# A gate's sum moved out of a prologue: ScalarE and GpSimd take it over beside the second half of v, and GpSimd alone splits the weight pieces

## The chip, the cores and the metric

The kernel runs on one core of one Trainium2 chip. The metric is the device time of one execution in microseconds (us). The engines, as the profile names them: PE is TensorE's matmuls and PEld its weight loads, DVE is VectorE, ACT is ScalarE, POOL is GpSimd, and SP is SyncE, which here only issues DMAs. Each engine runs its own instructions strictly in the order in which the program holds them, so an instruction that waits holds up everything behind it on that engine; this is the thing to keep in mind in what follows.

## The reference

Two attention blocks run on the same input x (2048 x 1024, f32), one linear (A) and one softmax (B), each with 32 heads of 32 columns, and a gate mixes them row by row:

```python
x = A_x
g = _sigmoid((x * gate_w).sum(-1, keepdims=True))
a = _A_ref(x, A_wqkv, A_wo)     # linear attention, then @ wo
b = _B_ref(x, B_wqkv, B_wo)     # softmax attention, then @ wo
return g * a + (1 - g) * b
```

The change concerns two small parts of it. One is g: a weighted sum over the 1024 columns of x, for each of 2048 rows. The other is a preparation of `B_wo`: sums and differences of its quarters, each of them split in two parts.

## The kernel before, in words

All matmuls take f32 numbers split in a high part (a cast to fp32r) and a low part (the rest), with three matmuls per product: high by high, high by low, low by high. `split` makes both parts: ScalarE casts, another engine subtracts. So each operand costs one ScalarE and one VectorE instruction of 128x512.

The program has two ages. In the **prologue** all orders are written by hand. It goes through x in two halves, J = 0 and J = 1. For each half, `v_pass` makes the first half of v for B (8 steps k, banks 0 to 7), and then eight calls of `quad` make q and k for B by a scheme with seven instead of eight products per 2x2 block (`product(0)` to `product(6)`, 12 matmuls each, in six PSUM banks in turn). VectorE joins the products (L494, L501 to L503, L507, L508, L511) and splits results and weights (L294). While one quad runs, `quad_weights` builds the seven weight operands of the next one in a ring of `RINGW` places (12 before). `load_quad` fetches raw weights for the quad after that. After every product `quad` calls `next(side)`, and that is one **turn** for everything that runs beside it:

- `quad_weights`, a step per turn;
- `spill_rest`, which writes x's parts to memory for later (tiles xs);
- `gate_`, the generator `gate()`: for each of 4 column blocks j and 8 row blocks k it loads a 128x512 tile of x into the one buffer `gate_x` (SyncE), two turns later multiplies it by a column of weights and adds it to `gate_sum` (VectorE, L376 for the first k, L378 for the other seven), and after eight of these sums over the partitions by four small matmuls with `ones` (L381);
- `parts`, the generator `wo_parts()`: 28 pieces of B's output weights. GpSimd loads raw tiles by its own DMA queue (L526), ScalarE casts the high part (L534), GpSimd subtracts for the low part (L535), and GpSimd stores both (L537). A piece starts every `PIECE_STEP` = 4.1 turns.

`gate_x`, `gate_sum` and the raw pieces lie in the big tile 15; the pieces' parts in `zrep`. What `gate()` has not finished when the last quad but one of J = 1 ends, it finishes there in one go (`for _ in gate_: pass`).

Then comes the **main loop**. From here on a planner in Python chooses, instruction by instruction, what PE does next, by modelled times `T`; `use` books a cost on an engine, `T["pe"]` is 0 at its start. It begins with the second half of v (16 units of 24 matmuls, each unit loading x's parts again as xh<-xs and big<-xs), beside the first head's maxima; then come the heads, in which PE, VectorE and GpSimd are all close to full.

Of the kernel before, what the change touches and what calls it, by code (L numbers as in the profile page):

```python
# [11 lines left out]
F32R = mybir.dt.float32r  # L12
AF = mybir.ActivationFunctionType
# [6 lines left out]
P = 128  # L20
# [19 lines left out]
NE = 3  # L40
AHEAD_X = 3
PIECE_STEP = 4.1
LATE = 1.0
MANUAL = {ET.PE, ET.DVE, ET.Activation, ET.SP, ET.Pool}
NMID = 13
# [3 lines left out]
def kernel(  # L49
# [34 lines left out]
    def f32r(ap):  # L84
        return ap.bitcast(F32R)
# [34 lines left out]
    def big_tile(i, dtype):  # L120
        return sb.tile([P, S], dtype, name=f"big{i}")

    big = [None if i in (15, 16, 17) else big_tile(i, F32R) for i in range(NBIG)]
# [42 lines left out]
    def dma(to, of):  # L166

        T["sp"] = max(T["sp"], T["pe"]) + DMA_ISSUE
        nc.sync.dma_start(to, of)  # L169
# [140 lines left out]
    for side in PLACES:  # L310
        side["X12"] = side["T4"]
    NQB = 6
    RINGW = [(18, 0), (18, 1), (19, 0), (19, 1), (14, 0), (14, 1), (20, 0), (20, 1), (17, 0), (17, 1), (16, 0),
             (16, 1)]
    NP = len(PRODUCTS)
    QUADS = 2 * NK // 2
    assert NK == 8 and NPAIR == 2
# [21 lines left out]
    def halves(t):  # L339
        return [t[:, i * C:(i + 1) * C] for i in range(t.shape[1] // C)]  # L340

    RAW_BIG = (17, 16, 15)
    assert not {b for b, _ in RINGW[:NK]} & set(RAW_BIG)
    raw_big = [halves(big_tile(b, F32)) for b in RAW_BIG]
    raw_a = [mid[5], extra] + halves(sb.tile([P, 2 * HK * P], F32, name="xh"))
# [13 lines left out]

    def vcols(c):  # L360
        return [(2 * D + c * C, C)]

    z0, z1, gate_sum, gate_x = raw_w0
    gate_wt = mneg[:, :NK]

    def gate():

        yield
        for j in range(NJ):
            for k in range(NK):  # L370
                dma(gate_x, xT[k * P:(k + 1) * P, j * C:(j + 1) * C])
                yield
                yield
                w = gate_wt[:, k:k + 1]
                if k == 0:
                    nc.vector.tensor_scalar_mul(gate_sum, gate_x, w)  # L376
                else:
                    nc.vector.scalar_tensor_tensor(gate_sum, gate_x, w, gate_sum, op0=ALU.mult, op1=ALU.add)  # L378
                yield
            for i in range(TPC):  # L380
                nc.tensor.matmul(bank[7][:, i:i + 1], gate_sum[:, i * P:(i + 1) * P], ones[:, :1], start=True, stop=True)  # L381
            nc.scalar.activation(g_sb[:, j * TPC:(j + 1) * TPC], bank[7][:, :TPC], AF.Exp, scale=-1.0)
        nc.vector.tensor_scalar_add(g_sb, g_sb, 1.0)
        nc.vector.reciprocal(g_sb, g_sb)
        nc.vector.tensor_scalar(omg_sb, g_sb, -1.0, 1.0, op0=ALU.mult, op1=ALU.add)

    gate_ = gate()

    def load_x(raws, J, jj, k, c0=0, c1=C):
        j = 2 * J + jj  # L390
# [54 lines left out]
    def quad_weights(raws, J, f):  # L445

        w11, w12, w21, w22 = raws

        def part(s, raw):
            n = quad_ring(J, f, s)  # L450
            split(ring_w(n, 0), ring_w(n, 1), raw, nc.vector)

        part(0, w11)
        yield
        part(6, w22)
        nc.vector.tensor_add(w22, w21, w22)
        yield
        nc.vector.tensor_sub(w21, w11, w21)
        part(1, w12)
        nc.vector.tensor_sub(w11, w22, w11)  # L460
        yield
        part(3, w22)
        nc.vector.tensor_sub(w12, w12, w11)
        yield
        part(4, w11)
        part(2, w12)
        yield
        part(5, w21)
# [49 lines left out]

    def wo_parts():

        hi_w, lo_w = (f32r(z) for z in halves(zrep))
        at, turn = [1.0], count()

        def load(z, m, i, **add):
            if i < KH:
                nc.gpsimd.dma_start(z, wo_piece(m, i), **add)  # L526

        def wait():
            at[0] += PIECE_STEP
            while next(turn) + 1 < at[0]:  # L530
                yield

        def part(m, i, z):
            nc.scalar.copy(hi_w, z)  # L534
            nc.gpsimd.tensor_sub(lo_w, z, f32(hi_w))  # L535
            for p, src in enumerate((hi_w, lo_w)):
                nc.gpsimd.dma_start(wo_d[m][p][:, i * C:(i + 1) * C], f32(src))  # L537

        yield
        load(z1, "W11", 0)  # L540
        load(z0, "W21", 0)
        yield from wait()
        for i in range(KH):
            part("W11", i, z1)
            nc.gpsimd.tensor_sub(z1, z1, z0)
# [22 lines left out]
    parts = wo_parts()  # L568

    def halves_of(t):  # L570
        return [t[:, i * D:(i + 1) * D] for i in range(2)]
# [74 lines left out]
    for k in range(NK):  # L646
# [16 lines left out]
        if k == 6:  # L663
            for _ in spill(0, "X12"):
                pass
    for i, b in enumerate((16, 17)):
        w_t[i] = big[b] = big_tile(b, F32R)
    quad_w = quad_weights(raw_a, 0, 0)
    for _ in range(3):
        next(quad_w)  # L670
# [6 lines left out]

    def change():

        load_wv_again(range(NK - 3))  # L680
        split_x(raw_x1[0], 1, 0, 0)
        yield
        load_wv_again([NK - 3])
        split_x(raw_x1[0], 1, 1, 0)
        yield
        load_wv_again([NK - 2])
        split_x(raw_x1[0], 1, 0, 1)
        yield
        load_wv_again([NK - 1])
# [12 lines left out]
    for k in range(NK):  # L702
# [310 lines left out]
    def linear():  # L1013
        extra = iter(())
        for n, (i, t) in enumerate(units):
# [64 lines left out]
            if kind == "v":  # L1080
                give(b, use("act", 0.5, T["pe"] + LATENCY["pe"]))
                v_out(c, token(i, t), ps, mid[11 - n % 2])
            elif kind == "kv":
                va = mid[7][:, (n % 2) * HC:(n % 2 + 1) * HC]
                yield from keys_alone(n - 2)
                nc.scalar.copy(va, ps[:, HC:])
# [732 lines left out]
    while streams or tasks:  # L1819
        if not begun[0] and lin_done[0] >= warm and s_done[0] >= NT * NJ + LEAD:  # L1820
            begun[0] = True
            advance("head")
        pump_w()
        fold_now()
        add_now()
        load_w_op()
        fill(T["pe"] + SLACK)
        task = next((i for i, (start, _) in enumerate(tasks)
                     if start() is not None and start() <= T["pe"]), None)
        if task is not None:  # L1830
# [36 lines left out]
        advance(name)  # L1867
        goal[0] += (st_done[0] - before) * rates[lin_kind[0]]
# [24 lines left out]
```

## Time and profile before

| | |
|---|---|
| Median of 3 runs | 2891.49 us (2888.26 to 2895.98) |
| Profiled execution | 2892.11 us, of which the span of the profile is 2890.3 us |
| Granted TensorE clock, mean | 0.989 |
| Share of the span busy | PE 98%, DVE 81%, POOL 70%, ACT 56% |
| Bytes moved | 459.51 MB, mean 159 GB/s |

How to read it: a window row gives, for a stretch of time, each engine's busy time and in brackets its number of instructions, then the granted clock and the mean busy share of the 16 DMA engines. A row of the waits says who waited, for whom, how long in total, how many times, and the longest. PE's records overlap, since matmuls are pipelined; so PE's count in a stretch says more than its busy time. The prologue lies between 0 and some 480 us, the second half of v between 480 and 590 us, and the heads follow.

### The profile page before, as it was taken

The page shows a single profiled execution, that of the slowest core. Times are in us where ns is not written, and L with a number is a line of the kernel's source. Part 1 is how long each engine was busy: PE and PEld are TensorE (multiplying, and loading weights), DVE is VectorE, ACT ScalarE, POOL GpSimd, SP SyncE. Part 2 cuts the span into 40 slices and gives each one's busy share as a digit, 9 for nine tenths or more (in the row PEclk, how much of TensorE's full clock was granted, in tenths as well). Part 3 has the DMA queues.
Part 4 walks back from the last instruction along what each step waited for, and adds up shares of the span by engine and source line. Part 5 has one row for each costly group of instructions (what it writes and reads, how often), then busy time and mean ns, then how long its engine had stood idle before and what let it go on. Part 6 is the DMA issues. An engine that isn't in the chain of part 4 may idle for free.

```text
span 2890.3 us, 46884 instructions
## 1 busy us (share of the span) xinstructions
PE 2819.5 (98%) x15880; PEld 2055.3 (71%) x15880; DVE 2341.8 (81%) x3777; ACT 1630.6 (56%) x3063; POOL 2036.4 (70%) x1066
## 2 busy tenths in 40 slices
PE   9798888999999999999999999999999999999999
PEld 8677777876777677667766777777767666676677
DVE  7777665688888888888888888888888888887678
ACT  5334322066667566666666666666666666665522
POOL 0323303069899999999999999789989988888000
PEclk9899999999999999999999999999999999999999
DMA  8888876643443334434443344446656554644775
GB/s 278 268 255 272 271 217 200 186 137 105 101 126 103 95 96 119 114 98 108 113 116 92 96 108 133 151 152 201 189 172 198 153 155 112 173 116 131 249 245 156
DMA packets 403338, 459.51 MB, mean 159 GB/s; under 512 B 106894, under 2 KB 234894, under 8 KB 401308
## 3 DMA queue, kind: packets, MB, share of 16 engines
q1 hardware_dynamic: 381084, 419.03, 48.2%
q0 software_dynamic: 22016, 37.50, 6.0%
q8 instruction: 126, 2.06, 0.3%
q14 instruction: 112, 0.92, 0.1%
HBM read 314.31 MB, written 127.66 MB: 153 GB/s over the span
## 4 chain that ended last, share of the span: by engine, by line
PE 84%; DMA 7%; DVE 5%; issue 2%; ACT 2%; SPq 1%; POOL 0%; ACTq 0%; DVEq 0%
PE bank L1350 16%; PE bank L1208 16%; PE bank L1500 15%; PE bank L152 11%; PE bank L155 11%; PE bank L157 11%; DMA big<-in_xT 2%; DVE big L294 2%; DMA qk<-mid 1%; ACT mid L293 1%; SPq L169 1%; DVE mid L294 1%; DMA xh<-in_b_wqkv 1%; PE bank L1272 1%; DMA v<-mid 1%
## 5 line engine op out<-in xcount | busy, mean ns | idle before, releaser
L1435 POOL TENSOR_TENSOR big<-big,big 128x512 f32<-128x512 f32 (+2 forms) x694 | 1642.5, 2371 | 107.5 <-ACT big L1353 64.8
L1213 DVE TENSOR_REDUCE mx<-bank 128x1 f32<-128x512 f32 x2048 | 1313.4, 683 | 297.4 <-PE bank L1208 294.0
L1353 ACT ACTIVATE big<-bank 128x512 f32<-128x512 f32 x2048 | 1180.5, 602 | 429.3 <-PE bank L1350 363.2
L1350 PE MATMUL bank<-big,big 128*128 128x512 f32 x1888 | 741.5, 394 | 2.2 <-DMA big<-ml 1.6
L1208 PE MATMUL bank<-big,big 128*128 128x512 f32 x1888 | 739.2, 392 | 1.7 <-ACT big L1353 1.7
L152 PE MATMUL bank<-big,big 128*128 128x512 f32 x1576 | 625.2, 397 | 33.9 <-DVE mid L503 21.3
L155 PE MATMUL bank<-big,big 128*128 128x512 f32 x1576 | 621.7, 394 | 1.3 <-DVE big L294 1.1
L157 PE MATMUL bank<-big,big 128*128 128x512 f32 x1572 | 619.4, 394 | 0.3 <-DMA big<-xs 0.2
L1500 PE MATMUL bank<-big,mid 128*32 128x512 f32 x4096 | 454.2, 593 | 0.0
L1350 PEld LDWEIGHTS bank<-big,big 128*128 128x128 f32 x1888 | 354.0, 188 | 127.2 <-issue 47.0
L1208 PEld LDWEIGHTS bank<-big,big 128*128 128x128 f32 x1888 | 354.5, 188 | 75.7 <-ACT big L1353 3.4
L152 PEld LDWEIGHTS bank<-big,big 128*128 128x128 f32 x1576 | 300.7, 191 | 104.4 <-issue 24.5
L155 PEld LDWEIGHTS bank<-big,big 128*128 128x128 f32 x1576 | 300.8, 191 | 65.4 <-DVE big L294 2.3
L157 PEld LDWEIGHTS bank<-big,big 128*128 128x128 f32 x1572 | 299.3, 190 | 65.7 <-DMA big<-xs 1.2
L1500 PEld LDWEIGHTS bank<-big,mid 128*32 128x32 f32 x4096 | 143.5, 110 | 264.4 <-issue 264.1
L1451 DVE TENSOR_TENSOR bank<-bank,big 128x512 f32<-128x512 f32 x364 | 251.8, 692 | 5.2 <-ACT big L1353 2.9
L535 POOL TENSOR_TENSOR zrep<-big,zrep 128x512 fp32r<-128x512 f32 x28 | 40.6, 1449 | 230.3 <-ACT zrep L534 191.7
L293 ACT CAST mid<-mid 128x512 fp32r<-128x512 f32 x64 | 39.7, 620 | 207.9 <-DVE mid L503 103.2
L1431 POOL TENSOR_TENSOR big<-big,big 128x1536 f32<-128x1536 f32 (+1 forms) x31 | 123.2, 3975 | 40.6 <-ACT big L1353 40.4
L294 DVE TENSOR_TENSOR big<-mid,big 128x512 fp32r<-128x512 f32 (+1 forms) x157 | 111.8, 727 | 47.3 <-ACT big L293 47.1
L152 PE MATMUL bank<-big,xh 128*128 128x512 f32 x376 | 147.1, 391 | 0.7 <-DVE mx L1213 0.7
L293 ACT CAST big<-mid 128x512 fp32r<-128x512 f32 (+1 forms) x157 | 92.7, 617 | 96.0 <-DVE mid L1619 66.0
(154 smaller groups left out, 2284.1 us busy)
## 6 DMA issues: line engine op xcount, KB each, us to landing
big<-xs SPq DMA_DIRECT2D x288, 256.0 KB
big<-qk SPq DMA_DIRECT2D x690, 64.0 KB
xh<-xs SPq DMA_DIRECT2D x144, 256.0 KB
qk<-mid SPq DMA_DIRECT2D x128, 256.0 KB
big<-oA SPq DMA_DIRECT2D x84, 256.0 KB
xs<-big SPq DMA_DIRECT2D x64, 256.0 KB
oA<-mid SPq DMA_DIRECT2D x64, 256.0 KB
big<-big POOLq DMA_DIRECT2D x50, 256.0 KB, 5.5
```

The source lines that it names most:

```text
L152: yield nc.tensor.matmul(ps, sh, mh_, start=(kt == 0), stop=False)
L155: yield nc.tensor.matmul(ps, sh, ml_, start=False, stop=(late and last))
L157: yield nc.tensor.matmul(ps, sl, mh_, start=False, stop=last)
L293: nc.scalar.copy(hi, src)
L294: eng.tensor_sub(lo, src, f32(hi))
L1208: nc.tensor.matmul(bank[b], q[:, t % TPC * P:(t % TPC + 1) * P], k[:, j * C:(j + 1) * C], start=True, stop=True)
L1213: nc.vector.tensor_reduce(m[:, t, j:j + 1], bank[b], AX.X, ALU.max)
L1350: nc.tensor.matmul(bank[b], k[:, t * P:(t + 1) * P], q_cols(h, j), start=True, stop=True)
L1353: nc.scalar.activation(pr_t[i][:, j * C:(j + 1) * C], bank[b], AF.Exp, scale=SCALE)
L1435: nc.gpsimd.tensor_add(lacc[:, sl], lacc[:, sl], pr(t)[:, sl])
L1451: nc.vector.tensor_add(lacc[:, qp:] if t == NT - 1 else l_b[:, :n], l_b[:, :n], src)
L1500: nc.tensor.matmul(av_b[j * DH:(j + 1) * DH, :], v[:, t, :], pr(t)[:, j * C:(j + 1) * C], start=(t == 0), stop=(t == NT - 1))
```

## The change

Two steps move.

1. `gate()` goes. Its work is done by `gate_step()`, which the main loop calls once per decision: from `T["pe"]` = 8.0 on, one step each 2.5 modelled us, 32 steps. A step loads a tile of x (SyncE) into one of four buffers; 8 us later ScalarE multiplies it by its weight column, and GpSimd adds it to one of two sums. The matmuls with `ones` remain, four groups of four, as tasks of the planner.
2. In a piece, GpSimd casts the high part itself. ScalarE only writes one column of a small tile, from which GpSimd copies, so that a piece still starts where it did. The raw tiles move to `zrep`, the parts to half of big 15; that frees one more place for the ring `RINGW`, which becomes 13 long.

With the longer ring `quad_weights` makes its operands up to a turn earlier: operand 6 and the sum behind it in the first turn, and so on. And the reload of the v weights (`load_wv_again`) takes six instead of five steps in its first turn.

```diff
-    RINGW = [(18, 0), (18, 1), (19, 0), (19, 1), (14, 0), (14, 1), (20, 0), (20, 1), (17, 0), (17, 1), (16, 0),
-             (16, 1)]
+    RINGW = [(16, 0), (16, 1), (17, 0), (17, 1), (19, 0), (19, 1), (14, 0), (14, 1), (20, 0), (20, 1), (15, 0),
+             (18, 0), (18, 1)]
...
-    RAW_BIG = (17, 16, 15)
+    RAW_BIG = (20, 15, 18)
...
-    def gate():
-        yield
-        for j in range(NJ):
-            for k in range(NK):
-                dma(gate_x, xT[k * P:(k + 1) * P, j * C:(j + 1) * C])
-                yield
-                yield
-                w = gate_wt[:, k:k + 1]
-                if k == 0:
-                    nc.vector.tensor_scalar_mul(gate_sum, gate_x, w)
-                else:
-                    nc.vector.scalar_tensor_tensor(gate_sum, gate_x, w, gate_sum, op0=ALU.mult, op1=ALU.add)
-                yield
-            for i in range(TPC):
-                nc.tensor.matmul(bank[7][:, i:i + 1], gate_sum[:, i * P:(i + 1) * P], ones[:, :1], start=True, stop=True)
...
         part(0, w11)
-        yield
         part(6, w22)
         nc.vector.tensor_add(w22, w21, w22)
         yield
         nc.vector.tensor_sub(w21, w11, w21)
         part(1, w12)
+        yield
         nc.vector.tensor_sub(w11, w22, w11)
+        part(3, w22)
         yield
-        part(3, w22)
         nc.vector.tensor_sub(w12, w12, w11)
+        part(4, w11)
         yield
-        part(4, w11)
         part(2, w12)
...
-        hi_w, lo_w = (f32r(z) for z in halves(zrep))
+        z0, z1 = halves(zrep)
+        hi_w, lo_w = (big[15][:, i * C:(i + 1) * C] for i in (2, 3))
...
         def part(m, i, z):
-            nc.scalar.copy(hi_w, z)
+            n = next(tokens) % (C // DH)
+            nc.scalar.copy(dn[0][:, n:n + 1], eps)
+            nc.gpsimd.tensor_copy(dn[1][:, n:n + 1], dn[0][:, n:n + 1])
+            nc.gpsimd.tensor_copy(hi_w, z)
             nc.gpsimd.tensor_sub(lo_w, z, f32(hi_w))
...
+    gate_wt = omg_sb[:, :NK]
+    gate_n, gate_at, gate_busy = [0], [GATE_FROM], deque()
+    gate_x = [mid[7], mid[8], mid[9], zrep[:, :C]]
+    def gate_step():
+        while gate_busy and min(gate_busy)[0] <= T["pe"]:
+            first = min(gate_busy)
+            gate_busy.remove(first)
+            first[-1]()
+        n = gate_n[0]
+        if n >= NJ * NK or gate_at[0] > T["pe"]:
+            return
+        gate_n[0] += 1
+        gate_at[0] = T["pe"] + GATE_STEP
+        j, k = divmod(n, NK)
+        raw, acc = gate_x[n % len(gate_x)], (mid[6], zrep[:, C:])[j % 2]
+        assert all(at[1] > n - len(gate_x) for at in gate_busy)
+        dma(raw, xT[k * P:(k + 1) * P, j * C:(j + 1) * C])
+        def times():
+            use("act", 0.62, T["pe"])
+            nc.scalar.activation(raw if k else acc, raw, AF.Copy, scale=gate_wt[:, k:k + 1])
+            if k:
+                plus()
+        def plus():
+            end = use("pool", 1.3, T["act"] + LATENCY["act"])
+            nc.gpsimd.tensor_add(acc, acc, raw)
...
+        gate_busy.append((T["pe"] + 8.0, n, times))
...
-    quads(0, lambda: load_pair(raw_x1[0], 1, 0), spill_rest(0), gate_, parts)
+    quads(0, lambda: load_pair(raw_x1[0], 1, 0), spill_rest(0), parts)
...
-    quads(1, lambda: load_v1(raw_a, range(KH)), spill_rest(1), gate_, parts)
-    for _ in gate_:
-        pass
+    quads(1, lambda: load_v1(raw_a, range(KH)), spill_rest(1), parts)
...
         pump_w()
+        gate_step()
```

Three places show what this does to the order. The first is VectorE in a quad of J = 0, around the join of product 4 (in the rows before, L463 is the last sum of `quad_weights`, L378 the gate's step, L501 to L503 the join). Before:

```order
L294 TENSOR_TENSOR big_223<-xh,big_223 128x512
L456 TENSOR_TENSOR xh<-xh 128x512
L458 TENSOR_TENSOR xh<-mid_229,xh 128x512
L294 TENSOR_TENSOR big_221<-extra,big_221 128x512
L460 TENSOR_TENSOR mid_229<-xh,mid_229 128x512
L294 TENSOR_TENSOR big_222<-xh,big_222 128x512
L463 TENSOR_TENSOR extra<-extra,mid_229 128x512
L378 SCALAR_TENSOR_TENSOR big_250<-big_250,mneg 128x512
L501 TENSOR_TENSOR mid_234<-bank_239,mid_226 128x512
L502 TENSOR_TENSOR mid_235<-bank_238,mid_234 128x512
```

The same place now, with the changed program's line numbers (L438 is the last sum, L476 and L477 the join):

```order
L295 TENSOR_TENSOR big_614<-extra,big_614 128x512
L435 TENSOR_TENSOR mid_229<-xh,mid_229 128x512
L295 TENSOR_TENSOR big_221<-xh,big_221 128x512
L438 TENSOR_TENSOR extra<-extra,mid_229 128x512
L295 TENSOR_TENSOR big_221<-mid_229,big_221 128x512
L476 TENSOR_TENSOR mid_234<-bank_239,mid_226 128x512
L477 TENSOR_TENSOR mid_235<-bank_238,mid_234 128x512
```

Nothing that waits for a load of x stands ahead of the join any more, and one weight split (big_221<-mid_229) has come ahead of it.

The second place is the beginning of a piece on GpSimd. Before:

```order
L526 DMA big_250<-in_b_wo 128x512 x2
L535 TENSOR_TENSOR zrep<-big_250,zrep 128x512
L537 DMA woW_0_260<-zrep 128x512
L537 DMA woW_1_261<-zrep 128x512
L545 TENSOR_TENSOR big_250<-big_250 128x512
```

And now:

```order
L502 DMA zrep<-in_b_wo 128x512 x2
L512 COPY dn_205<-dn_204 128x1
L513 CAST big_613<-zrep 128x512
L514 TENSOR_TENSOR big_613<-zrep,big_613 128x512
L516 DMA woW_0_260<-big_613 128x512
L516 DMA woW_1_261<-big_613 128x512
L524 TENSOR_TENSOR zrep<-zrep 128x512
```

The cast of 128x512 has come to GpSimd, together with the copy of one column that waits for ScalarE; on ScalarE a copy of 128x1 stands where the cast stood.

The third place is SyncE's queue in the second half of v, from the second store of v on. Before:

```order
L169 DMA v_161<-mid_234 128x512
L169 DMA v_161<-mid_235 128x512
L169 DMA v_161<-mid_234 128x512
L169 DMA mid_226<-v_160 128x16x32
L169 DMA xh<-xs_13_76 128x512
L169 DMA xh<-xs_13_92 128x512
L169 DMA big_210<-xs_14_77 128x512
```

And now:

```order
L170 DMA v_161<-mid_234 128x512
L170 DMA mid_231<-in_xT 128x512
L170 DMA zrep<-in_xT 128x512
L170 DMA v_161<-mid_235 128x512
L170 DMA mid_231<-in_xT 128x512
L170 DMA mid_232<-in_xT 128x512
L170 DMA v_161<-mid_234 128x512
L170 DMA mid_226<-v_160 128x16x32
L170 DMA mid_233<-in_xT 128x512
L170 DMA xh<-xs_13_76 128x512
L170 DMA xh<-xs_13_92 128x512
```

The gate's loads (in_xT) now stand between the loads of x's parts (xs) that PE needs there. From the first heads on the order of all engines is what it was.

More of the change, by code (lines that the diff above doesn't have):

```diff
@@ L42 @@
 PIECE_STEP = 4.1
+GATE_STEP, GATE_FROM = 2.5, 8.0
 LATE = 1.0
@@ L121, in big_tile @@
         return sb.tile([P, S], dtype, name=f"big{i}")
-    big = [None if i in (15, 16, 17) else big_tile(i, F32R) for i in range(NBIG)]
+    big = [None if i in (15, 18, 20) else big_tile(i, F32R) for i in range(NBIG)]
     mid = [sb.tile([P, C], F32, name=f"mid{i}") for i in range(NMID)]
@@ L361, in vcols @@
         return [(2 * D + c * C, C)]
-    z0, z1, gate_sum, gate_x = raw_w0
-    gate_wt = mneg[:, :NK]
-    def gate():
-        yield
-        for j in range(NJ):
-            for k in range(NK):
-                dma(gate_x, xT[k * P:(k + 1) * P, j * C:(j + 1) * C])
-                yield
-                yield
-                w = gate_wt[:, k:k + 1]
-                if k == 0:
-                    nc.vector.tensor_scalar_mul(gate_sum, gate_x, w)
-                else:
-                    nc.vector.scalar_tensor_tensor(gate_sum, gate_x, w, gate_sum, op0=ALU.mult, op1=ALU.add)
-                yield
-            for i in range(TPC):
[L381 to L387, printed above, removed]
     def load_x(raws, J, jj, k, c0=0, c1=C):
@@ L519, in wo_parts @@
     def wo_parts():
-        hi_w, lo_w = (f32r(z) for z in halves(zrep))
-        at, turn = [1.0], count()
+        z0, z1 = halves(zrep)
+        hi_w, lo_w = (big[15][:, i * C:(i + 1) * C] for i in (2, 3))
+        at, turn, tokens = [1.0], count(), count()
         def load(z, m, i, **add):
@@ L568, with total @@
     parts = wo_parts()
+    gate_wt = omg_sb[:, :NK]
[23 more added lines that the diff above has]
+            nc.gpsimd.tensor_add(acc, acc, raw)
+            if k == NK - 1:
+                gate_busy.append((end + 0.5, NJ * NK, lambda: tasks.append((bank_at, total))))
+        def total():
+            b = take()
+            end = use("pe", 0.45, free[b])
+            for i in range(TPC):
+                nc.tensor.matmul(bank[b][:, i:i + 1], acc[:, i * P:(i + 1) * P], ones[:, :1], start=True, stop=True)
+            give(b, use("act", 0.2, end))
+            nc.scalar.activation(g_sb[:, j * TPC:(j + 1) * TPC], bank[b][:, :TPC], AF.Exp, scale=-1.0)
+            if j == NJ - 1:
+                nc.vector.tensor_scalar_add(g_sb, g_sb, 1.0)
+                nc.vector.reciprocal(g_sb, g_sb)
+                nc.vector.tensor_scalar(omg_sb, g_sb, -1.0, 1.0, op0=ALU.mult, op1=ALU.add)
+                use("dve", 0.4)
+                gate_n[0] += 1
+        gate_busy.append((T["pe"] + 8.0, n, times))
     def halves_of(t):
@@ L665 @@
                 pass
-    for i, b in enumerate((16, 17)):
-        w_t[i] = big[b] = big_tile(b, F32R)
+    for b in RAW_BIG:
+        big[b] = big_tile(b, F32R)
+    w_t[2] = big[18]
     quad_w = quad_weights(raw_a, 0, 0)
@@ L678, in change @@
     def change():
-        load_wv_again(range(NK - 3))
+        load_wv_again(range(NK - 2))
         split_x(raw_x1[0], 1, 0, 0)
         yield
-        load_wv_again([NK - 3])
+        load_wv_again([NK - 2])
         split_x(raw_x1[0], 1, 1, 0)
         yield
-        load_wv_again([NK - 2])
+        load_wv_again([NK - 1])
         split_x(raw_x1[0], 1, 0, 1)
         yield
-        load_wv_again([NK - 1])
         split_x(raw_x1[0], 1, 1, 1)
@@ L1083, in linear @@
             elif kind == "kv":
+                assert gate_n[0] > NJ * NK
                 va = mid[7][:, (n % 2) * HC:(n % 2 + 1) * HC]
```

## Prediction

> **What bounds the kernel now.** I read the page first, then a table of windows, then the waits of the prologue, then the chain of work that ended last at one of the stalls. A tenth of a percent of this kernel is 3 us; a difference of about 0.3% (9 us) is what a measurement can tell from no change.
>
> The page, its first part and its fourth:
>
> ```profile
> PE 2819.5 (98%) x15880; PEld 2055.3 (71%) x15880; DVE 2341.8 (81%) x3777; ACT 1630.6 (56%) x3063; POOL 2036.4 (70%) x1066
> PE 84%; DMA 7%; DVE 5%; issue 2%; ACT 2%; SPq 1%; POOL 0%; ACTq 0%; DVEq 0%
> ```
>
> PE bounds the whole, and 16% of the chain are not PE. The windows show where that lies:
>
> ```profile
> core 0: us, PE busy (x) PEld busy (x) DVE busy (x) ACT busy (x) POOL busy (x), PEclk, DMA share, GB/s
> 0.00:50.00 50.00, 48.82 (x210) 40.66 (x211) 40.06 (x66) 27.68 (x49) 1.96 (x8) 1.00 0.93 300
> 50.00:100.00 50.00, 46.33 (x205) 38.06 (x204) 34.48 (x50) 18.88 (x35) 8.90 (x10) 1.00 0.81 250
> 100.00:150.00 50.00, 36.46 (x140) 29.42 (x139) 34.28 (x49) 15.66 (x29) 15.92 (x21) 0.80 0.83 260
> 150.00:200.00 50.00, 49.77 (x220) 40.95 (x219) 37.59 (x51) 16.14 (x29) 15.07 (x18) 1.00 0.87 254
> 200.00:250.00 50.00, 39.37 (x155) 30.97 (x155) 36.98 (x49) 18.88 (x34) 18.93 (x24) 0.90 0.89 284
> 250.00:300.00 50.00, 42.51 (x184) 34.85 (x183) 33.81 (x44) 20.04 (x35) 20.70 (x25) 0.93 0.88 271
> 300.00:350.00 50.00, 45.93 (x194) 36.85 (x193) 37.21 (x51) 18.39 (x35) 14.53 (x17) 0.97 0.81 250
> 350.00:400.00 50.00, 39.91 (x156) 32.21 (x155) 32.89 (x50) 15.40 (x29) 5.20 (x6) 0.86 0.71 225
> 400.00:450.00 50.00, 50.00 (x222) 41.43 (x221) 37.22 (x58) 16.42 (x30) 0.00 (x0) 1.00 0.82 230
> 450.00:500.00 50.00, 41.18 (x173) 33.88 (x173) 23.19 (x39) 11.99 (x22) 25.15 (x38) 0.90 0.60 190
> ```
>
> An undisturbed window holds 222 matmuls (400 to 450), so one costs 50 / 222 = 0.225 us. A window's loss is 50 us less its count times 0.225. In the order of the rows that is 2.7, 3.8, 18.5, 0.5, 15.1, 8.6, 6.3, 14.9, 0.0 and 11.0 us, together 81.4 us. Part of it is clock: where PE stood for long, the granted clock falls to 0.80 to 0.90 of full over the window, and the matmuls after the stall run slow. So a stall costs more than its wait, and the count holds both.
>
> Who made PE wait, and who made those wait (waits of the first 640 us):
>
> ```profile
> PE bank L381 <- DVE big L378: 25.3, 3, 9.9
> PE bank L152 <- DVE mid L503: 21.3, 6, 7.3
> PE bank L152 <- ACT mid L357: 7.5, 1, 7.5
> DVE big L378 <- DMA big<-in_xT: 39.3, 18, 4.4
> ACT zrep L534 <- DMA woS<-zrep: 13.3, 5, 5.9
> ACT zrep L534 <- DMA woW<-zrep: 9.2, 2, 8.0
> ```
>
> The first line is the gate's own matmuls, waiting for the gate's sum. The second is PE waiting for a bank that VectorE empties late (L503). The fourth says why VectorE is late: it stands 39.3 us, 18 times, at the gate's step L378 until a tile of x has landed. The chain at the longest stall shows the whole mechanism:
>
> ```profile
> 127.31 3.96 DMA mid<-in_b_wqkv
> ...
> 134.46 5.79 DMA big<-in_xT
> 140.27 0.76 DVE big L378
> 141.03 0.04 issue
> 141.07 1.87 PE bank L381 x8
> ```
>
> One buffer, a load of 5.79 us begun only when the step before has read it, a VectorE step that waits for it in the middle of the quad's joins, and PE behind that.
>
> **The gate leaves the prologue.** Of the ten windows' losses I give the gate five. 3.8 us (50 to 100): PE stands once, at 90, behind the L378 of the first row below. 18.5 us (100 to 150): two stalls, the longest among them above. 14.9 us (350 to 400) and 11.0 us (450 to 500): the other two long L381 waits, and L503. For 200 to 250 the loss of 15.1 us has two halves: a wait of 7.3 us on L503, behind a tile of x, and after it a ScalarE wait of the pieces, which the change removes too. It is the 8.0 us above, the second row below:
>
> ```profile
> 90.14 0.75 DVE L378 SCALAR_TENSOR_TENSOR big<-big,mneg 128x512 f32<-128x512 f32 x1 [3.74 <-DMA big<-in_xT]
> 237.29 0.62 ACT L534 CAST zrep<-big 128x512 fp32r<-128x512 f32 x1 [8.02 <-DMA woW<-zrep]
> ```
>
> Sum: 3.8 + 18.5 + 15.1 + 14.9 + 11.0 = 63.3 us that can go. I leave the start (2.7), the 8.6 us of 250 to 300 (the 7.5 us behind ACT L357 are stores of v that wait for their own buffers, which the change does not touch), 6.3 us of 300 to 350, and 0.5. What is late next? With the gate's loads gone, the joins wait for PE. VectorE was busy 34 to 38 us of 50 in the quads' windows with the gate's steps in it. And the windows 150 to 200 and 400 to 450 show PE undisturbed with gate and pieces running, or with the gate alone, so nothing else in a quad is slower than PE's 84 matmuls (19 us). DMA is the one that could be: its share was 0.81 to 0.89 in the quads of J = 0, and the same bytes less the gate's come in less time. In 200 to 250 PE was at 155 of 222 with DMA at 0.89. Between nothing and 20 us (a third of the gain) for that I take 5 us, nearer to the window 150 to 200, where PE ran undisturbed at 0.87.
>
> The longer ring and the steps that come a turn earlier add no instruction. I cost them at nothing: operand 6 now overwrites what product 0 of the running quad has just read, so the casts wait for nothing that P1's copy ahead of them does not wait for. What covers them is that raw weights are loaded a quad (19 us) ahead; were these late, the first turn would wait for them, and that is part of the 20 us above. SyncE's queue, from which 32 loads go, holds up the stores and weight loads less.
>
> **The pieces on GpSimd.** 28 casts leave ScalarE, and with them its 22.5 us of waits for stores; 28 copies of one column come, too small to matter on an engine that is busy a third of the time. GpSimd gets 28 casts of 128x512. The rows, ScalarE's cast first and then the nearest on GpSimd:
>
> ```profile
> L534 ACT CAST zrep<-big 128x512 fp32r<-128x512 f32 x28 | 17.3, 617 | 22.6 <-DMA woS<-zrep 13.3 <-DMA woW<-zrep 9.2
> L535 POOL TENSOR_TENSOR zrep<-big,zrep 128x512 fp32r<-128x512 f32 x28 | 40.6, 1449 | 230.3 <-ACT zrep L534 191.7 <-DMA woW<-zrep 16.6 <-DMA woS<-zrep 11.3
> L545 POOL TENSOR_TENSOR big<-big 128x512 f32<-128x512 f32 x4 | 5.2, 1299 | 0.1
> L1095 POOL COPY mid<-mid 128x256 f32<-128x256 f32 x4 | 1.6, 396 | 0.0
> ```
>
> A copy of half the width takes 0.396 us, so a cast takes between that and a subtraction, 0.40 to 1.45 us; I take twice the copy, 0.8 us, and 28 x 0.8 = 22 us of GpSimd, which waited 230 us at L535 alone. Now GpSimd, not ScalarE, waits for a store before the parts are overwritten; behind it stand only later pieces. So nothing of this is on the path by itself. But GpSimd slows VectorE:
>
> ```profile
> L378 DVE SCALAR_TENSOR_TENSOR big<-big,mneg x28: 740/752/1825, 76.9 to 461.2; 128x512 f32<-128x512 f32 x28
> 76.95 1.82 DVE L378 SCALAR_TENSOR_TENSOR big<-big,mneg 128x512 f32<-128x512 f32 x1
> 76.91 1.31 POOL L535 TENSOR_TENSOR zrep<-big,zrep 128x512 fp32r<-128x512 f32 x1 [48.14 <-ACT zrep L534]
> ```
>
> The same instruction takes 0.752 us as a rule and 1.825 us at worst, and a slow one begins here 0.04 us after a GpSimd subtraction and ends 0.55 us after it. The excess is 1.07 us at most. If each cast held up one VectorE instruction so, that would be 28 x 1.07 = 30 us of VectorE; if none, nothing. VectorE has 12 us of 50 free and will not wait for x any more, so I take 5 us on the path. The Trainium skill ("SBUF — State Buffer", Who interferes with whom) speaks against the change here: a VectorE instruction with two SBUF inputs and a GpSimd instruction that reads SBUF exclude each other, and the later one blocks until the other ends. By that rule a cast blocks for its whole length, 28 x 0.8 = 22 us of VectorE, and with all of it on the path the forecast would be 17 us longer. The trace agrees in the one pair above (1.82 us where 0.75 is usual).
>
> **The gate in the second half of v.** 32 loads of 256 KB, 32 ScalarE steps, 28 GpSimd sums, and the same small matmuls:
>
> ```profile
> L381 PE MATMUL bank<-ones,big 128*128 128x1 f32 x32 | 6.6, 326 | 25.3 <-DVE big L378 25.3
> ```
>
> The matmuls' 6.6 us move and cost the same there. ScalarE's 32 x 0.62 = 20 us (priced as its cast above) and GpSimd's 28 x 1.30 = 36 us (as L545) go where both have room. The stage, then a load of x's parts from the chain and two issues from SyncE's timeline:
>
> ```profile
> 486.00:510.00 24.00, 24.00 (x107) 19.89 (x106) 1.72 (x3) 2.97 (x5) 14.79 (x27) 1.00 0.91 265
> 510.00:587.00 77.00, 76.88 (x339) 63.00 (x337) 53.96 (x80) 8.47 (x15) 0.00 (x0) 1.00 0.64 193
> 517.54 4.52 DMA big<-xs
> 536.28 0.80 SPq L169 DMA_DIRECT2D big<-xs x2
> 539.90 0.80 SPq L169 DMA_DIRECT2D xh<-xs x2
> ```
>
> ScalarE is busy 8.47 of 77 us, GpSimd 0. DMA is what fills up. At share 0.64 it moves 193 GB/s, so at 1.00 some 302. The 32 loads are 8.4 MB, 28 us of that. The stage's 101 us hold 0.91 x 24 + 0.64 x 77 = 71 us of DMA; with the loads 99 of 101. The loads of x's parts have little room in it. One half of a unit is issued each 3.6 us (536.28 to 539.90), into a buffer that is needed two halves, 7.2 us, later; issuing takes 0.80 and landing 4.52, which leaves 1.9 us. One or two of the gate's loads stand ahead of each pair in SyncE's queue (0.4 us to issue, 0.9 us of DMA each), and SyncE also waits there until GpSimd has added from the buffer that it loads again. That wait stands before x's parts, and PE waits behind it. On ScalarE the step waits for its tile ahead of the copies that empty v's banks; six banks in turn cover that for some units' time. Cost: nothing if the 1.9 us hold, 12 units that load x's parts, so 24 halves x 1 us = 24 us, if each is a microsecond late. I take 8 us, nearer to nothing, because the mean share stays below full and only the first 24 us are over it.
>
> **Sum.** 63.3 - 5 (DMA in the quads) - 5 (VectorE behind GpSimd) - 8 (v) = 45 us less. The profiled execution took 2892.1 us, 0.6 us over the median of the runs, so 2892.1 - 45.3 = 2846.8, and I give 2847.
>
> **Rivals.**
>
> *The stalls move instead of going.* DMA or SyncE's queue is the second to be late in the quads, and half of the 63.3 us comes back as waits for raw weights and for stores of q and k. For it: shares of 0.83 to 0.89 while PE ran at two thirds in 100 to 150 and 200 to 250. Against: 150 to 200. 2892.1 - 31.6 + 5 + 8 = 2873. Chance 0.17.
>
> *The second half of v becomes the bound, and the kernel is slower.* SyncE stands at a gate load until GpSimd has freed its buffer. This buffer's round (load 5.8 us, ScalarE 0.6, GpSimd 1.3, each in order behind other work) takes longer than the four steps (10 us) given to it, and the loads of x's parts behind it come late each time. It decides from (63.3 - 10) / 32 = 1.7 us lost per gate load. At 2.5 us each the stage grows by 80 us: 2892.1 - 53.3 + 80 = 2919. For it: DMA at 99 of 101 us. Against: the round adds up to 7.7 us, and GpSimd and ScalarE stand nearly empty there. Chance 0.05.
>
> *More goes than I count.* None of the three costs shows, and the 6.3 us of 300 to 350, where the gate runs too, go as well: 2892.1 - 69.6 = 2822. Chance 0.08.
>
> That the gate stays in the prologue is excluded by the order, in which L378 is gone from VectorE there.
>
> **How the numbers follow.** The forecast has 0.70, and its time is 2847: with the costs' lower ends it is 2829, and with 18 us more of them 2865. The range, 2822 to 2876, takes in the case where more goes and the case where stalls move; left out are the slower rival and the worst ends of the costs together. Faster by over 0.3%: 0.70 + 0.17 + 0.08 less 0.03 for costs that add up, 0.92. Within 0.3%: 0.03. Slower: 0.05.
>
> **What would show it.** Right: no PE wait on a gate's sum in the prologue; the waits on the joins (21.3 us) down to a few; the windows 100 to 150, 200 to 250 and 350 to 400 at 205 matmuls or more; the v stage longer by 5 to 12 us at a DMA share near 0.9. GpSimd's cast at 0.7 to 0.9 us. Wrong: windows of the quads still at 160 to 190 with DMA at 0.9 and over (the first rival), or PE waits on x's parts (xs) of over 40 us in v (the second).

## The result, and the profile after

The changed kernel takes 2838.95 us (median of 4 runs, 2838.61 to 2840.74), the kernel before, beside it on the same chip, 2889.88 us (2887.18 to 2895.98). The ratio is 0.9822, with a 95% interval of 0.9805 to 0.9839: 51 us or 1.8% faster. The forecast was 2847 us, in a range of 2822 to 2876.

The page after, its first part and its fourth (before: PE 2819.5, and 16% of the chain not PE):

```profile
PE 2804.4 (99%) x15880; PEld 2044.2 (72%) x15880; DVE 2332.1 (82%) x3745; ACT 1638.2 (58%) x3095; POOL 2108.2 (74%) x1150
PE 87%; DMA 4%; DVE 1%; issue 1%; ACT 0%; SPq 0%; POOL 0%; ACTq 0%; DVEq 0%; POOLq 0%
```

The windows after, the rows that answer to those of before:

```profile
core 0: us, PE busy (x) PEld busy (x) DVE busy (x) ACT busy (x) POOL busy (x), PEclk, DMA share, GB/s
...
100.00:150.00 50.00, 47.64 (x208) 38.51 (x206) 43.21 (x56) 16.36 (x34) 28.36 (x37) 1.00 0.98 299
150.00:200.00 50.00, 48.33 (x204) 39.26 (x205) 42.82 (x55) 17.88 (x37) 24.46 (x33) 0.97 0.81 261
200.00:250.00 50.00, 46.37 (x200) 36.92 (x199) 40.09 (x49) 18.20 (x36) 29.56 (x37) 1.00 0.86 285
250.00:300.00 50.00, 40.51 (x168) 32.62 (x167) 33.22 (x45) 19.43 (x39) 20.30 (x26) 0.90 0.86 269
300.00:350.00 50.00, 49.92 (x221) 40.88 (x220) 42.98 (x61) 17.43 (x35) 17.14 (x22) 1.00 0.89 277
350.00:400.00 50.00, 50.00 (x222) 41.42 (x221) 39.84 (x63) 18.93 (x35) 0.00 (x0) 1.00 0.74 232
...
450.00:500.00 50.00, 45.41 (x197) 37.07 (x196) 28.13 (x41) 14.45 (x25) 20.64 (x16) 0.93 0.86 265
```

100 to 150 went from 140 matmuls to 208, 350 to 400 from 156 to 222, and the clock there is full again. 150 to 200 lost 16 of its 220 and 250 to 300, which holds v's stores, 16 of its 184; as the kernel is ahead by then, a row no longer holds quite the same work as the row of before. The waits of the first 640 us after:

```profile
PE bank L153 <- ACT mid L358: 9.4, 1, 9.4
PE bank L153 <- DMA xh<-xs: 4.6, 1, 4.6
PE bank L153 <- DVE mid L478: 4.0, 4, 2.2
PE bank L1234 <- ACT big L1379: 1.4, 1, 1.4
PE bank L158 <- DVE big L295: 1.4, 1, 1.4
```

The gate's sum (25.3 us before) is gone from the list, and the joins fell from 21.3 us to 4.0 (L478, before L503). The first row is the old one of v's stores, 9.4 us where it was 7.5. The second is new; its cause stands in the chain there, in the first third of the stage with v's second half:

```profile
435.57 10.63 DMA mid<-in_xT
446.20 0.02 issue
446.23 0.73 ACT mid L571
...
447.09 1.31 POOL mid L577
448.40 0.07 issue
448.47 1.29 POOL mid L577
449.76 1.36 SPq L170
...
451.23 5.43 DMA xh<-xs
456.66 0.04 issue
456.70 0.79 PE bank L153
```

A gate's tile lands after 10.63 us, ScalarE multiplies, GpSimd adds, SyncE may load that buffer again only now, and x's parts (xs), for which PE waits, stand behind that load in SyncE's queue.

To split the time by stage I use two marks on PE: the start of the matmul that begins the second half of v (486.0 us before; the 1733rd, not counting the gate's own and the first 16, which only warm PE up) and of the one behind its last unit (598.9 us, the 2210th). These come from one profiled execution for each kernel; two executions of the changed kernel gave 423.2 and 427.5 us for the first mark, so differences under some 5 us in one mark say little.

| Kernel | quads end, us | v's second half, us | ratio to before (95%) |
|---|---|---|---|
| before | 486.0 | 112.9 | 1 |
| after | 423.2 | 122.9 | 0.9822 (0.9805 to 0.9839) |
| after, run again (e10) | 427.5 | 122.4 | 0.9827 (0.9813 to 0.9842) |
| e1: before + casts on GpSimd | 484.2 | 113.8 | 0.9993 (0.9983 to 1.0002) |
| e2: before, no gate | 417.1 | 112.9 | 0.9766 (0.9750 to 0.9782) |
| e3: before, gate's steps, one load | 452.4 | 114.2 | 0.9882 (0.9868 to 0.9897) |
| e4: before, gate's loads, 4 steps | 426.3 | 113.0 | 0.9792 (0.9778 to 0.9807) |
| e5: after, casts on ScalarE | 421.4 | 122.4 | 0.9808 (0.9793 to 0.9822) |
| e6: after, no gate | 426.0 | 113.0 | 0.9795 (0.9779 to 0.9811) |
| e9: before + gate moved to v | 416.6 | 121.7 | 0.9803 (0.9786 to 0.9821) |
| e11: no gate, ring of 13 alone | 419.7 | 112.7 | 0.9770 (0.9754 to 0.9786) |
| e12: no gate, GpSimd's casts alone | 421.4 | 111.7 | 0.9771 (0.9757 to 0.9786) |

The whole gain lies ahead of the heads: the quads end 62.8 us earlier, v takes 10.0 us longer, and the span is 53.2 us shorter.

### The profile page after: what moved, and what is told of

It reads as the page before. It is cut to its first block, busy times and chain, and to the rows that moved or that the text cites. A ratio compares the mean times of both kernels' runs of the same rounds, so it can differ in the third digit from the quotient of the medians.

```text
span 2837.1 us, 47025 instructions
## 1 busy us (share of the span) xinstructions
PE 2804.4 (99%) x15880; PEld 2044.2 (72%) x15880; DVE 2332.1 (82%) x3745; ACT 1638.2 (58%) x3095; POOL 2108.2 (74%) x1150
## 4 chain that ended last, share of the span: by engine, by line
PE 87%; DMA 4%; DVE 1%; issue 1%; ACT 0%; SPq 0%; POOL 0%; ACTq 0%; DVEq 0%; POOLq 0%
PE bank L1376 17%; PE bank L1234 16%; PE bank L1526 16%; PE bank L153 12%; PE bank L156 12%; PE bank L158 12%; DVE big L295 1%; DMA mid<-in_xT 1%; PE bank L1298 1%; DMA xh<-xs 1%; DMA big<-wv 1%; PE bank L1023 1%; PE bank L912 0%; DMA big<-ra 0%; DMA qk<-mid 0%
## 5 line engine op out<-in xcount | busy, mean ns | idle before, releaser
L295 DVE TENSOR_TENSOR big<-mid,big 128x512 fp32r<-128x512 f32 (+1 forms) x157 | 121.1, 787 | 44.5 <-ACT big L294 44.3
L153 PE MATMUL bank<-big,xh 128*128 128x512 f32 x376 | 148.1, 394 | 5.3 <-DMA xh<-xs 5.3
L158 PE MATMUL bank<-big,xh 128*128 128x512 f32 x376 | 147.8, 393 | 0.0
L156 PE MATMUL bank<-big,xh 128*128 128x512 f32 x376 | 147.7, 393 | 0.0
```

The source lines that it names most:

```text
L153: yield nc.tensor.matmul(ps, sh, mh_, start=(kt == 0), stop=False)
L156: yield nc.tensor.matmul(ps, sh, ml_, start=False, stop=(late and last))
L158: yield nc.tensor.matmul(ps, sl, mh_, start=False, stop=last)
L295: eng.tensor_sub(lo, src, f32(hi))
```

## The experiments

**What the gate costs in the prologue, and by what.** My theory was that the wait for a tile in one buffer is what costs; the rival, that VectorE's own steps (or the loads' bytes) do. First the gate was left out (g filled with 0.5; the load of its weights went too, which the cut below does not show):

```diff
-    gate_ = gate()
+    nc.vector.memset(g_sb, 0.5)
+    nc.vector.memset(omg_sb, 0.5)
+    gate_ = iter(())
```

> The kernel before without the gate's sum: no loads, no VectorE steps, no small matmuls, the gate's two tiles are filled with 0.5. It gives the whole price of the gate in the prologue. By the prediction's steps 63.3 us less the pieces' share of some 5 us: 55 to 60 us less than before. If the stalls moved instead of going (the first rival): 25 to 35 us less.

Measured: 2823.65 us, ratio 0.9766. The gate's price is 68.9 us at the quads' end, more than expected. Then its two halves apart. All 32 steps, with one tile loaded once (so that the other sums read a stale tile):

```diff
-                dma(gate_x, xT[k * P:(k + 1) * P, j * C:(j + 1) * C])
+                if j == k == 0:
+                    dma(gate_x, xT[k * P:(k + 1) * P, j * C:(j + 1) * C])
```

> The kernel before with all 32 VectorE steps and the small matmuls of the gate, but only the first of the 32 loads (the steps read the same tile again). If the waits for loads were the price: within 10 us of the kernel without a gate. If VectorE's own work (26 us of steps) was the price: no more than 25 us less than before.

And all 32 loads, with only the first step of each column block (so that a sum has one term):

```diff
-                else:
-                    nc.vector.scalar_tensor_tensor(gate_sum, gate_x, w, gate_sum, op0=ALU.mult, op1=ALU.add)
```

> The kernel before with all 32 loads of the gate, but only the 4 first steps of the 32 on VectorE (k = 0); the sum is left out. If VectorE's waits for loads were the price, 28 of 32 go: 45 us less than before or more. If the 8.4 MB of DMA and SyncE's queue were the price: no more than 20 us less.

Measured: 2857.87 us for the steps alone, 37 us less than before and so between its two expectations, and 2832.83 us for the loads alone. By the first mark the loads alone cost 426.3 - 417.1 = 9.2 us, the steps alone 452.4 - 417.1 = 35.3 us, and the remaining 24.4 of the 68.9 us exist only where a step waits for a load. Both kernels keep the gate's 16 small matmuls, four groups that each hold PE's stream up by some 0.8 us in the trace of the loads alone, so their 3.3 us are counted twice, and the part that needs both is nearer to 28 us. Either way the theory that the load is all of it falls: steps that wait for no load cost PE about half of the price. The waits of the kernel with the steps alone show on what:

```profile
PE bank L382 <- DVE big L379: 15.8, 3, 8.9
PE bank L152 <- ACT mid L357: 11.3, 1, 11.3
PE bank L152 <- DVE mid L504: 3.1, 3, 2.3
```

and its chain at the longest of the three stalls:

```profile
126.53 0.60 DVE mid L461
127.13 0.07 DVE big L294
...
127.65 0.68 DVE extra L464
128.34 1.71 DVE big L379
130.04 0.04 issue
130.09 1.86 PE bank L382 x8
```

VectorE's steps L379 never wait for a tile there. It is late with the sum because it has the quad's weights and joins to make first, and because this step takes 1.71 us where the median of the 28 is 0.744: a subtraction of GpSimd runs beside it, from 127.69 to 129.48. The four matmuls of the gate (two records each) stand in PE's order at a fixed place, so PE waits for the sum though nothing else needs it. In the window from 100 to 150 this kernel runs 166 matmuls at a granted clock of 0.86.

**The pieces.** GpSimd's casts were added to the kernel before, without the rest of the change:

```diff
-            nc.scalar.copy(hi_w, z)
+            n = next(tokens) % (C // DH)
+            nc.scalar.copy(dn[0][:, n:n + 1], eps)
+            nc.gpsimd.tensor_copy(dn[1][:, n:n + 1], dn[0][:, n:n + 1])
+            nc.gpsimd.tensor_copy(hi_w, z)
```

> The kernel before with the second step of the change alone: GpSimd casts the pieces, ScalarE writes one column; the gate stays in the prologue. If the gate's waits are the cause, only ScalarE's 22.5 us of waits for the pieces' stores go, of which 8.0 us stood on the path: 3 to 8 us less than before. If the pieces carried the gain: 25 us less or more. If GpSimd's casts cost VectorE more than they save: up to 10 us more than before.

and, the other way round, the cast was given back to ScalarE in the changed kernel:

> The changed kernel with the pieces' cast back on ScalarE (no column copies), the gate in v as changed, the pieces' tiles as changed. If ScalarE's waits for the pieces' stores are worth what the prediction gave them: 3 to 8 us more than the changed kernel. If GpSimd's casts hold VectorE up as much as they save: the same within 3 us.

Measured: ratio 0.9993 and 0.9808. Added alone the casts bring nothing, and taken back they cost nothing (0.9808 against 0.9822, intervals that overlap). So to take ScalarE's 22.5 us of waits for the pieces' stores away is worth nothing on balance. The window from 200 to 250, of which I had given half to such a wait of 8.0 us, still holds only 181 matmuls with the casts on GpSimd (155 before):

```profile
200.00:250.00 50.00, 43.81 (x181) 35.68 (x180) 35.01 (x48) 15.16 (x32) 25.61 (x35) 0.90 0.91 297
```

What it gains there is lost again from 250 on: 350 to 400 falls from 156 to 134. Without the gate, but with the casts still on ScalarE (e2), the two windows hold 200 and 222, as many as in the changed kernel. Both windows are the gate's.

**What the other parts of the change cost.** The changed kernel without its gate (g filled with 0.5; the pieces, the ring and the order as changed):

```diff
-    gate_n, gate_at, gate_busy = [0], [GATE_FROM], deque()
+    gate_n, gate_at, gate_busy = [NJ * NK + 1], [GATE_FROM], deque()
+    nc.vector.memset(g_sb, 0.5)
+    nc.vector.memset(omg_sb, 0.5)
```

> The changed kernel without the gate's sum (no loads, no steps, no small matmuls; the two tiles are filled with 0.5). It gives the gate's price in the second half of v. By the prediction 8 us less than the changed kernel; from the profile of the changed kernel, in which PE waits 4.6 us for x's parts at 456 and runs slow after it, 6 to 8 us less. If the stage hides the gate: the same within 2 us.

Measured: 2833.75 us, ratio 0.9795. Against the changed kernel v is 122.9 - 113.0 = 9.9 us shorter, so that is what the gate costs there. But the quads end at 426.0, 8.9 us later than in the kernel before without its gate. Three kernels part this: the gate's move alone, on the kernel before (as in the diff above the prediction, without the hunks on the ring, `quad_weights` and the pieces), and, without any gate, the ring with its earlier steps (and the tiles and the reload that go with it) alone and the casts alone.

> The kernel before with one part of the change alone: the gate's 32 steps leave the prologue for the last half of v, on ScalarE and GpSimd as in the changed kernel. The pieces' cast stays on ScalarE, the ring of weight parts keeps 12 places and the quads' steps their order. Theory A (the longer ring with its steps a turn earlier, or GpSimd's casts, cost the 10 us by which the changed kernel without its gate, 2833.8, lies above the kernel before without its gate, 2823.7): 2823.7 + 5 to 8 us for the gate in v = 2829 to 2832, faster than the changed kernel by 7 to 10 us. Theory B (they cost nothing, the 10 us lie between chips): the time of the changed kernel, 2837 to 2841. PE's lost time up to 620 us 35 us by A, 42 us or more by B.

> The changed kernel without the gate (filled with 0.5) and with the pieces' cast on ScalarE: of the change only the ring of 13 places and the steps that come a turn earlier are left. Theory A1 (the ring and its order cost the 10 us): 2831 to 2835. Theory A2 (GpSimd's casts cost them) or B (nothing does): 2822 to 2826.

> The kernel before without the gate (filled with 0.5) and with the pieces' cast on GpSimd behind a one-column token: of the change only that is left; the ring has 12 places. Theory A1 (the ring and its order cost the 10 us): 2822 to 2826. Theory A2 (GpSimd's casts cost them, since they hold up VectorE): 2831 to 2835. Theory B (nothing does): 2822 to 2826, with the ring's kernel at the same time.

The changed kernel ran beside them on the same chip:

> The changed kernel as it is, timed beside the others on the same chip: 2837 to 2841 us by every theory.

Measured, in this order: 2837.15, 2827.15, 2827.62 and 2843.63 us. None of the theories holds as it was put. That one part costs all 10 us falls: ring alone (0.9770) and casts alone (0.9771) lie between the kernel without either (0.9766) and with both (0.9795), and the single differences are no larger than the intervals. The same holds at the first mark: 2.6 and 4.3 us, 8.9 us together. Beyond the 5 us of scatter only the two together show, and even their two kernels (e2 and e6) ran on different chips, with intervals that touch. PE's waits for VectorE's joins point the same way: 4.3 us with both (e6), 0.6 with the ring alone, 0.2 with the casts alone. That nothing costs them (theory B, 2837 to 2841 us for the gate's move alone) fits 2837.15 as a number, but not the run of the changed kernel beside it, nor the first mark.

With the gate's move alone the quads end at 416.6 us, as early as without any gate. Its four runs (2831.08 to 2840.14 us) lie below the four of the changed kernel (2841.77 to 2844.39 us) on that chip. The medians differ by 6.5 us, 0.2%, and the ratios' intervals just overlap, so it is the best version seen here, by a difference at the edge of what these runs can tell.

What the two parts do is seen on VectorE. I took its sums and differences of two SBUF tiles between 60 and 340 us from the traces and sorted them by what GpSimd did at the same time (mean us of one, count in brackets):

| Kernel | GpSimd idle | beside a cast or copy of GpSimd | beside a two-input operation of GpSimd | sum over 0.686 us |
|---|---|---|---|---|
| before | 0.687 (149) | | 1.175 (45) | 22 us |
| before, no gate (e2) | 0.686 (177) | | 1.140 (49) | 22 us |
| ring alone (e11) | 0.686 (169) | | 1.242 (54) | 30 us |
| casts alone (e12) | 0.686 (122) | 0.703 (55) | 1.484 (43) | 35 us |
| after | 0.685 (106) | 0.700 (61) | 1.555 (49) | 43 us |

The 21 us of VectorE that the changed kernel loses more stand in the column of the two-input operations, all of them subtractions for the pieces. An instruction that met a cast and then the subtraction behind it is in that column too: 14 of the 49, which lost 4.7 us, while the 35 that met no cast lost 37.9. The ring adds 8 of the 21 us, the casts 13, and both add up. What is left open is why VectorE meets these subtractions at a worse moment with the longer ring; I made no run on that.

**What is left.** Two attempts on the two longest stalls that remain. The gate's steps later in v, so that the first loads of x's parts are through:

```diff
-GATE_STEP, GATE_FROM = 2.5, 8.0
+GATE_STEP, GATE_FROM = 2.2, 22.0
```

> The changed kernel with the gate's steps from 22.0 on instead of 8.0, each 2.2 instead of 2.5: the stage's first 24 us, in which DMA is full with stores of q and k and loads for the heads, are left to them. If the stall at 456 comes from the gate's loads in that stretch: 4 to 8 us less than the changed kernel. If the gate's loads cost the same wherever they stand: the same within 2 us.

Measured: 2841.11 us, ratio 0.9823 (0.9808 to 0.9838), no difference. And the first four copies of v's results ahead of most of the next quad's weights on ScalarE:

```diff
-            next(quad_w)
-        elif k == 6:
-            for _ in quad_w:
-                pass
...
+        if t == TPC:
+            for _ in quad_w:
+                pass
```

> The changed kernel with ScalarE's first four copies of v out of the banks moved ahead of all but the first step of the next quad's weights. In the changed kernel PE waits 9.4 us at 266 for these copies, which stand on ScalarE behind casts that wait for raw weights. If that order is the cause: 6 to 9 us less than the changed kernel. If the copies' own buffers (their stores) are the cause: the same within 2 us.

Measured: 2845.28 us, ratio 0.9832 (0.9817 to 0.9847), not faster. In both the stalls only came at other places. With the later steps PE waits 5.2 us for x's parts in v, in five places and never over 2.0 us, instead of 4.9 us in two. With the earlier copies the one stall of 9.4 us becomes two, 2.7 and 5.4 us: the first four copies begin at 258 instead of 265, but the next ones then wait 6.7 us for a store of v to free their buffer (4.1 us in the changed kernel). So neither the order nor the buffers alone set that stall; no run changed both.

## Why the prediction was right

**63.3 us that can go.** Nearly right in size: the price is 68.9 us by the kernel without any gate, and 69.4 (486.0 - 416.6) went with the gate's move alone. The 62.8 us of the whole change are already less what the pieces and the ring cost. Counting lost matmuls per window, clock and all, found it, where the two rows of waits on VectorE add up to 25.3 + 21.3 = 46.6 us. Part of the attribution was wrong: the 8.0 us wait of ScalarE at 237 us, which I gave to the pieces, was worth nothing (e1).

**The mechanism.** Half right. I put all of it on the load of 5.79 us in one buffer. Loads alone cost 9.2 us, steps alone 35.3, and the wait of the one for the other 24.4. That the change takes all three away at once is why this error did not show in the time; to that extent the number was luck. A second buffer for the tile might so have saved 24 to 28 us, over a third of the price; that was not tried.

**DMA in the quads, 5 us.** Not seen in the quads themselves. With the gate's move alone the window from 100 to 150 ran undisturbed at a share of 0.98:

```profile
100.00:150.00 50.00, 50.00 (x222) 41.45 (x221) 41.12 (x61) 19.67 (x35) 18.97 (x25) 1.00 0.98 317
```

**VectorE behind the casts, 5 us, and the ring, nothing.** Together they took 6.6 us (423.2 against 416.6; 10.9 by the second execution, 8.9 without the gate), against 5 in the sum. That the sum comes out is partly luck, since it gave the ring no part. GpSimd's cast is the 0.8 us that I took for it only by the mean, 22.2 us over all 28; the median is 0.616 us, and the long ones, up to 1.124 us, begin while a VectorE instruction with two SBUF inputs runs:

```profile
L513 POOL CAST big<-zrep x28: 608/616/1124, 75.2 to 328.3; 128x512 fp32r<-128x512 f32 x28
```

And VectorE loses little to the casts themselves, 5.5 us in all (4.7 as above, and 0.8 where it met a cast alone). It is the subtraction that GpSimd now begins right behind its cast that meets VectorE. GpSimd's and VectorE's timelines after, at one piece:

```profile
103.06 1.09 POOL L513 CAST big<-zrep 128x512 fp32r<-128x512 f32 x1
104.23 1.61 POOL L514 TENSOR_TENSOR big<-zrep,big 128x512 fp32r<-128x512 f32 x1
```

```profile
102.99 0.69 DVE L295 TENSOR_TENSOR big<-mid,big 128x512 fp32r<-128x512 f32 x1
103.59 1.10 DVE L435 TENSOR_TENSOR mid<-mid,mid 128x512 f32<-128x512 f32 x1
104.62 1.78 DVE L295 TENSOR_TENSOR big<-mid,big 128x512 fp32r<-128x512 f32 x1
```

The cast ends at 104.15, the VectorE instruction beside it at 104.69; the subtraction ends at 105.84, VectorE's next at 106.40: each VectorE instruction ends 0.54 to 0.56 us after the one of GpSimd that it met, and the cast itself takes 1.09 us for 0.61. The Trainium skill ("SBUF — State Buffer", Who interferes with whom) says that such a pair blocks in the order of starting, for the whole length of the first; these rows agree. The 22 us of VectorE that I worked out from it for the casts did not come: they lost VectorE 5.5 us. That 21 us more were lost over both parts is a coincidence, since these stand beside the subtractions and 8 of them come with the ring. The quads end later by a third to a half of the 21 us. The ring, costed at nothing, had its part in it.

**The gate in v, 8 us.** Right: 10.0 us, and 8.8 to 9.9 us in the other two pairs (e9 against e2, after against e6). The mechanism was the one told, a load of x's parts behind a gate's load in SyncE's queue that waits for GpSimd, but it struck once and not at each load. By the starts of PE's matmuls the stage holds one wait of 4.6 us at 456, 2.8 us for the 13 matmuls behind it, which begin 0.43 us apart and more where 0.23 is usual, and 3.2 us for the gate's own small matmuls, four groups of 0.8, which moved here from the quads; together that is 10.6 us. The tile at that wait took 10.63 us to land, where the forecast reckoned with a load of 5.8 us. The stage filled up as forecast. Nearly all of it after:

```profile
430.00:545.00 115.00, 108.97 (x480) 88.56 (x478) 58.10 (x88) 34.46 (x60) 45.11 (x45) 0.97 0.87 271
```

0.87 x 115 is 100 us of DMA, where the forecast had 99; the stage grew, so that the share stays under full. 10.0 us over 32 loads is 0.3 us each; the slower rival needed 1.7.

**The sum.** In the order of the forecast, 63.3 - 5 - 5 - 8 = 45.3, the marks give 69.4 - 0 - 6.6 - 10.0 = 52.8: 8 us less than the forecast, most of it the DMA that was not late and the 69.4 us for 63.3. Of the rival in which stalls move, half of the 63.3 us coming back, there is only the wait of 4.6 us in v and 1.9 us more at v's stores. The slower 150 to 200 is not of it: with the gate's move alone that window holds 222, so it belongs to the pieces and the ring. The rival in which more goes came close in the quads alone (it had 69.6 us go there, and 69.4 went with the gate's move alone), but its costs showed.

**What would show it.** No wait on the gate's sum, few on the joins: yes. 205 matmuls in three windows: 208, 200 and 222, so one missed. The pieces and the ring are not why: the window holds 201 with the gate's move alone and 200 without any gate. In these two PE waits there for a weight of v (0.8 and 0.5 us) and for a cast (1.8 and 2.8 us), in the pass for v's first half. The cast at 0.7 to 0.9 us: 0.79 by the mean, 0.616 by the median.

## What to carry to other kernels

Work that nothing needs soon is not free because it is small: at a fixed place in the order of two engines, 32 steps of 0.75 us cost PE 35 us even with their data there, and the waits for loads in front of them 24 us or more on top. Count what a stall costs in lost matmuls per window, not in its wait, and when a step has two suspects, run each alone before choosing the remedy. Of a change with several parts, run the parts: here the gate's move alone came out 0.2% lower than the whole, at the edge of what these runs can tell.

## What the runs showed of the hardware

A DMA share of 0.98 over 50 us (317 GB/s) went with an undisturbed PE at 222 matmuls; I had taken shares of 0.9 for a warning. A stall costs PE more than its wait: in the kernel with the gate's steps alone, the rows of waits that are the gate's (15.8 and 3.1 us) add up to 19 us, and the quads end 35 us later than without the gate. The gate's own matmuls are some 3 us of that, and part is the clock, granted at 0.86 in the window of the longest stall: behind it the 12 matmuls from 132.81 to 137.50 start 0.43 us after one another, where 0.23 is usual, which is 2.4 us. And a cast of GpSimd with one input was held up by VectorE as a subtraction is (1.09 us for 0.61), while VectorE lost only 0.4 us to it (1.10 for 0.69) and 1.1 us to the subtraction (1.78).
